# Loading k in 2 KB packets, like q, and turning it back on TensorE: a retention layer with routing on one Trainium2 core

## The chip, the cores and the metric

The kernel runs on one core of one Trainium2 chip. The metric is device time in microseconds (us) of one execution; lower is better. The engines are TensorE (PE in the profile, its weight loads PEld), VectorE (DVE), ScalarE (ACT), GpSimd (POOL) and SyncE (SP). SP issues most of the transfers, POOL the weight loads and the indirect transfers.

## The reference

Inputs are q, k and v, each 4 x 8 x 768 x 64 in float32 (4 batches, 8 heads, 768 tokens, head size 64), a gate vector of 512 and two weight matrices of 512 x 1024 and 1024 x 512. First comes a recurrent attention, then a small feed-forward network on the 128 best-scored tokens of each batch:

```python
gamma = 1.0 - 2.0 ** (-5.0 - np.arange(H))
for t in range(S):
    state = gamma * state + k_t (outer) v_t
    y[:, :, t] = scale * q_t @ state
# x = y with the heads side by side: (4, 768, 512)
scores = x @ w_gate
for b in range(B):
    top = the 128 tokens of the batch with the highest score
    h = relu(x[b, top] @ w1)
    out[b, top] = x[b, top] + sigmoid(scores[b, top]) * (h @ w2)
```

## The kernel before, in words

**Blocks.** A batch of 768 tokens is cut into 3 blocks of 256 tokens, which makes 12 blocks, m = 0 to 11. A block holds two chunks of 128 tokens, u = 0 and 1. The recurrence is computed by chunks: the scores of q and k inside a chunk, masked to the causal half and multiplied with v (`inside`), plus q times the state that the earlier chunks left (`across`). The state is kept in PSUM and a chunk's k and v are added to it (`update`); ScalarE copies it to SBUF for the next chunk.

**Loads.** `load(m)` issues on SP's queue, for one block, first q, then k, then v. q comes with 8 tokens of one head side by side in a partition, as runs of 8 x 64 float32, in two transfers (one for each parity of the head). k and v come with 2 tokens side by side, runs of 2 x 64 float32, in one transfer each. The pool `loads` has 5 buffers of each; blocks 0 to 3 are loaded ahead of the loop, block m + 4 at the start of iteration m.

**Casts.** `cast(m)` runs on POOL: q times its decay factors to `qb` (L184), k to bfloat16 `kb` (L186), v times its factors to `vb` (L187), in that order; iteration m casts block m + 2. The three results live in the pool `nats` with 5 buffers.

**Transposes.** `transposes(m, "q")` and `transposes(m, "k")` turn eight 128 x 128 tiles each on PE into the one PSUM tile `pt` (L196, L203; one buffer), and ScalarE copies it to `qT` (L198) or `kT` (L205). q's copy also sorts its tokens into natural order. k's layout, token pairs s and parity j, serves both as it is: `kb` has the tokens in the partitions, which is what the state update wants (L260), and `kT` has the head dimension there, which the scores want (L217).

**Scores.** `scores(m, part)` makes the products of four heads in the PSUM tile `pa` (one buffer), and DVE multiplies it with the causal mask into `am` (L220). `finish` copies the outputs to `xo` on ScalarE (L274) and forms the tokens' gate scores on DVE (`junk`, L277). `put` stores xo from SP's queue.

**Routing.** For each batch the rank of each token among all 768 is counted: `route_spread` (PE), `route_beats` (DVE comparisons, L312 to L319, into the tile `beats`), `route_ranks` (PE sums into two PSUM tiles `pk`), `route_index` (DVE; the tokens' numbers go into the tile `idx`, L354). Then `route_fetch` gathers the 128 rows with an indirect transfer on POOL (L360), `route_gate`, `route_turn` and `route_sigmoid` make the gate and the transposed rows, `ffn_up` and `ffn_down` are the network, `ffn_add` sums (L423), and `route_put` scatters the rows back with an indirect transfer on POOL (L428), which reads `idx` again. `idx`, `acc` and `gt` come from the pool `perb`, which has 2 buffers, so batch 2 takes the buffers of batch 0. The tiles of `route_spread`, `route_ranks`, `route_turn`, `ffn_up` and `ffn_down` share the tag "pm" of the PSUM pool `psM`, which has 2 buffers taken in turn.

**Order.** The order is written out by hand: each engine executes its instructions in the order of the program. The routing parts are put into numbered places of the iterations:

```python
for m in range(NBLK):
    load(m + 4); slot_work(m, -1); cast(m + 2)
    transposes(m + 1, "q"); scores(m, 1); update(m, 0)
    slot_work(m, 0); transposes(m + 1, "k"); slot_work(m, 1)
    py = inside(m); across(m, 0, py); across(m, 1, py)
    xo = finish(m, py); update(m, 1); put(m, xo)
    slot_work(m, 2); scores(m + 1, 0); slot_work(m, 3); slot_work(m, 4)
```

Batch b ends with block 3b + 2; its ranks are in place 3 and its index in place 4 of iteration 3b + 3. For batch 0 the fetch is in iteration 5 (place -1), the gate, turn and sigmoid in 7, the network in 8, the sum in 9 and `route_put(0)` in iteration 10 (place -1); batch 1 runs three iterations later, and batches 2 and 3 end in the places that follow the loop.

Of the kernel before, what the change touches and what calls it, by code (L numbers as in the profile page):

```python
# [9 lines left out]
FT = mybir.dt.float32  # L10
# [8 lines left out]
def kernel(ctx: ExitStack, tc: tile.TileContext, q, k, v, w_gate, w1, w2, capacity, out):  # L19
    nc = tc.nc  # L20
# [18 lines left out]
    consts = ctx.enter_context(tc.tile_pool(name="consts", bufs=1))  # L39
    loads = ctx.enter_context(tc.tile_pool(name="loads", bufs=5))  # L40
    work = ctx.enter_context(tc.tile_pool(name="work", bufs=3))
    nats = ctx.enter_context(tc.tile_pool(name="nats", bufs=5))
    store = ctx.enter_context(tc.tile_pool(name="store", bufs=4))
    perb = ctx.enter_context(tc.tile_pool(name="perb", bufs=2))
    psT = ctx.enter_context(tc.tile_pool(name="psT", bufs=1, space=bass.MemoryType.PSUM))
# [11 lines left out]
    def load(m):  # L57
        b, r = divmod(m, NM)
        for nm, src in (("q", q), ("k", k), ("v", v)):
            ap = src[b, :, r * T:(r + 1) * T, :]  # L60
            if nm == "q":
                t = loads.tile([128, 2, 8, D], FT, name="qf", tag="qf")
                for half in range(2):
                    nc.sync.dma_start(t[:, half].rearrange("p j d -> p (j d)"),
                                      bass.AP(tensor=ap.tensor, offset=ap.offset + half * S * D,
                                              ap=[[8 * D, T // 8], [2 * S * D, HP], [1, 8 * D]]))
            else:
                t = loads.tile([128, H, 2, D], FT, name=nm + "f", tag=nm + "f")
                ap = bass.AP(tensor=ap.tensor, offset=ap.offset, ap=[[2 * D, 128], ap.ap[0], [1, 2 * D]])
                nc.sync.dma_start(t.rearrange("p h j d -> p h (j d)"), ap)  # L70
            raw[nm, m] = t
# [106 lines left out]

    def cast(m):
        r = m % NM  # L180
        kb = nats.tile([128, 2, H, D], BF, name="kb", tag="kb")
        vb = nats.tile([128, 2, H, D], BF, name="vb", tag="vb")
        qb = nats.tile([128, 8, 2, D], BF, name="qb", tag="qb")
        nc.gpsimd.tensor_mul(qb, raw["q", m].rearrange("p h j d -> p j h d"),  # L184
                             gq[:, r, :, :, None].to_broadcast([128, 8, 2, D]))
        nc.gpsimd.tensor_copy(kb, raw["k", m].rearrange("p h j d -> p j h d"))  # L186
        nc.gpsimd.tensor_mul(vb, raw["v", m].rearrange("p h j d -> p j h d"),  # L187
                             gv[:, 2 * r:2 * r + 2, :, None].to_broadcast([128, 2, H, D]))
        nat[m] = (kb, vb, qb)

    def transposes(m, nm):
        src = nat[m][2 if nm == "q" else 0]
        if nm == "q":
            pt = psT.tile([128, 8, T // 8, HP], BF, name="pt", tag="pt")
            for i in range(8):
                nc.tensor.transpose(pt[:, i].rearrange("p s g -> p (s g)"), src[:, i], ident)  # L196
            t = work.tile([128, HP, T], BF, name="qT", tag="qT")
            nc.scalar.activation(t.rearrange("p g (s i) -> p g s i", i=8), pt.rearrange("p i s g -> p g s i"), AF.Copy)  # L198
        else:
            pt = psT.tile([128, 2, HP, 128], BF, name="pt", tag="pt")  # L200
            for j in range(2):
                for dd in range(HP):
                    nc.tensor.transpose(pt[:, j, dd, :], src[:, j, 2 * dd:2 * dd + 2, :], ident)  # L203
            t = work.tile([128, 2, HP, 128], BF, name="kT", tag="kT")
            nc.scalar.activation(t, pt, AF.Copy)  # L205
        tr[nm, m] = t

    def scores(m, part):
        qT, kT = tr["q", m], tr["k", m]
        pa = psA.tile([128, 2, 2, 2, C], FT, name="pa", tag="pa")  # L210
        for d in range(2):
            dd = 2 * part + d
            for j in range(2):
                for u in range(2):
                    for half in range(2):
                        r = slice(half * 64, half * 64 + 64)
                        nc.tensor.matmul(pa[u * 64:u * 64 + 64, half, d, j, :], kT[r, j, dd, u * 64:u * 64 + 64],  # L217
                                         qT[r, dd, u * C:(u + 1) * C], start=True, stop=True)
        am = work.tile([128, 2, 2, 2, C], BF, name="am", tag=f"am{part}")
        nc.vector.tensor_mul(am.rearrange("p a b c d -> p (a b) (c d)"), pa.rearrange("p a b c d -> p (a b) (c d)"),  # L220
                             causal.rearrange("p a b -> p (a b)")[:, None, :].to_broadcast([128, 4, 2 * C]))
        att[m, part] = am
# [24 lines left out]
    def update(m, u):  # L247
        i = 2 * m + u
        b, c = divmod(i, NC)
        if c == NC - 1:  # L250
            return
        kb, vb, _ = nat[m]
        if c == 0:
            pstate[b] = psS.tile([128, HP, D], FT, name="pst", tag="pst")
        r = slice(u * 64, u * 64 + 64)
        for dd in range(HP):
            for j in range(2):
                for half in range(2):
                    h = 2 * dd + half
                    nc.tensor.matmul(pstate[b][half * 64:half * 64 + 64, dd, :], kb[r, j, h, :], vb[r, j, h, :],  # L260
                                     start=(c == 0 and dd == 0 and j == 0), stop=True, skip_group_check=True)
        t = S_sb[(i + 1) % 2]
        for half in range(2):
            r = slice(half * 64, half * 64 + 64)
            nc.scalar.activation(t[r, :, half * 64:half * 64 + 64], pstate[b][r], AF.Copy)  # L265
# [26 lines left out]
    def route_spread(b, r):  # L292
        st = batch[b]
        if r == 0:
            st["row"] = perb.tile([128, S - T], FT, name="row", tag="row")
            st["beats"] = perb.tile([128, NC, S], BF, name="beats", tag="beats")
            st["won"] = perb.tile([128, NC], FT, name="won", tag="won")
        pr = psM.tile([128, 2, C], FT, name="pr", tag="pm")
        for u in range(2):
            c = 2 * r + u  # L300
            nc.tensor.transpose(pr[:, u, :], st["sc"][:, c:c + 1].to_broadcast([128, C]), identf)
        st["pr"] = pr
        if r < NM - 1:
            nc.scalar.activation(st["row"][:, r * T:(r + 1) * T], pr.rearrange("p u t -> p (u t)"), AF.Copy)
# [40 lines left out]

    def route_index(b):
        st = batch[b]
        acc = perb.tile([128, 2], FT, name="acc", tag="acc")
        for a, (lo, hi, pk) in enumerate(st["pk"]):
            junk = store.tile([128, 4 * C], BF, name="junki", tag="junki")  # L350
            nc.vector.scalar_tensor_tensor(junk[:, :(hi - lo) * C], pk.rearrange("p a t -> p (a t)"), slotcol[:, 0:1],
                                           tokrow[:, lo * C:hi * C], OP.is_equal, OP.mult, accum_out=acc[:, a:a + 1])
        idx = perb.tile([128, 1], I32, name="idx", tag="idx")
        nc.vector.tensor_scalar(idx, acc[:, 0:1], acc[:, 1:2], float(b * S), OP.add, OP.add)  # L354
        st["idx"] = idx

# [30 lines left out]
    def route_sigmoid(b):  # L387
        st = batch[b]
        if b < B - 1:
            ssel = perb.tile([128, 1], FT, name="ssel", tag="ssel")  # L390
            nc.scalar.activation(st["prod"], st["prod"], AF.Copy, accum_out=ssel)
        else:
            ssel = st["ssel"]
        e = perb.tile([128, 1], FT, name="e", tag="e")
        nc.scalar.activation(e, ssel, AF.Exp, scale=-1.0)
        e1 = perb.tile([128, 1], FT, name="e1", tag="e1")
        nc.vector.tensor_scalar_add(e1, e, 1.0)
        gt = perb.tile([128, 1], FT, name="gt", tag="gt")
        nc.vector.reciprocal(gt, e1)
        st["gate"] = gt  # L400

# [62 lines left out]
    transposes(0, "q")  # L464
    transposes(0, "k")
    scores(0, 0)

    for m in range(NBLK):
        if m + 4 < NBLK:
            load(m + 4)  # L470
        slot_work(m, -1)
        if m + 2 < NBLK:
            cast(m + 2)
        if 1 <= m < 5:
            load_weights(m - 1)
        if m + 1 < NBLK:
            transposes(m + 1, "q")
        scores(m, 1)
        update(m, 0)
        slot_work(m, 0)  # L480
        if m + 1 < NBLK:
            transposes(m + 1, "k")
        slot_work(m, 1)
        py = inside(m)
        for u in range(2):
            across(m, u, py)
        xo = finish(m, py)
        update(m, 1)
        put(m, xo)
        slot_work(m, 2)  # L490
        if m + 1 < NBLK:
            scores(m + 1, 0)
        slot_work(m, 3)
        slot_work(m, 4)
    for t, place in sorted(slots):
# [36 lines left out]
```

## Time and profile before

| | |
|---|---|
| median of 3 runs | 128.45 us (126.95, 132.09, 128.45) |
| profiled execution | 127.14 us, of which the span of instructions is 125.4 us |
| busy share of the span | PE 65%, PEld 51%, DVE 60%, ACT 53%, POOL 62% |
| moved by transfers | 29.87 MB, mean 238 GB/s; 34,273 packets |
| mean granted TensorE clock | 0.866 |

Busy is the time in which an engine executes something; an engine's idle time is put down to what ended it (the releaser). A window's row lists each engine's busy time in that stretch with the number of instructions, the granted clock, the mean busy share of the 16 DMA engines (over 1 when packets overlap) and the rate. "SPq" and "POOLq" are the queues' issuing instructions.

### The profile page before, as it was taken

How to read it: one execution, taken by the hardware profiler on the slowest of the kernel's cores; microseconds unless marked ns; L12 is line 12 of the kernel's file. 1: busy time of each engine (PE TensorE's matmuls, PEld its weight loads, DVE VectorE, ACT ScalarE, POOL GpSimd, SP SyncE). 2: the span in 40 equal slices, each digit the busy share in tenths (PEclk: the TensorE clock that was granted, in tenths of full speed). 3: DMA queues.
4: the chain of work that ended last, by engine and by line, in shares of the span. 5: the costliest groups of instructions: out<-in, count | busy, mean ns of one | idle time of the engine just before them, and what ended most of it. 6: DMA issues, size and time to landing. Idle time of an engine off the chain costs nothing. (4 is left out here: it accounts for less than half of the span.)

```text
span 125.4 us, 3891 instructions
## 1 busy us (share of the span) xinstructions
PE 81.3 (65%) x1605; PEld 64.0 (51%) x1612; DVE 75.1 (60%) x217; ACT 66.3 (53%) x129; POOL 77.3 (62%) x72
## 2 busy tenths in 40 slices
PE   0053775958499729349939499995438697785820
PEld 0041655847487518238637398664326683462600
DVE  6002353789899958708948668599165864934120
ACT  7133474987657739307619869467607543430500
POOL 6649999999853798480699969848940300330330
PEclk9999997799859995865799859999965579999995
DMA  2999999999999999999999999999406104203202
GB/s 63 282 335 304 344 304 324 310 309 317 246 310 257 368 295 255 337 244 325 363 336 314 334 351 332 299 315 391 170 25 200 56 5 167 84 0 84 84 0 84
DMA packets 34273, 29.87 MB, mean 238 GB/s; under 512 B 1360, under 2 KB 26960, under 8 KB 34256
## 3 DMA queue, kind: packets, MB, share of 16 engines
q1 hardware_dynamic: 32016, 25.43, 66.8%
q0 software_dynamic: 2240, 4.20, 14.8%
q8 instruction: 12, 0.20, 0.6%
q14 instruction: 5, 0.04, 0.1%
HBM read 24.38 MB, written 7.34 MB: 253 GB/s over the span
## 5 line engine op out<-in xcount | busy, mean ns | idle before, releaser
L220 DVE TENSOR_TENSOR am<-pa,causal 128x1024 bf16<-128x1024 f32 x24 | 29.3, 1222 | 23.6 <-PE pa L217 23.6
L187 POOL TENSOR_TENSOR vb<-vf,gv 128x1024 bf16<-128x1024 f32 x12 | 22.8, 1900 | 9.3 <-DMA vf<-in_v_dram 9.1
L184 POOL TENSOR_TENSOR qb<-qf,gq 128x1024 bf16<-128x1024 f32 x12 | 22.8, 1902 | 6.6 <-DMA qf<-in_q_dram 4.8
L198 ACT ACTIVATE qT<-pt 128x1024 bf16<-128x1024 bf16 x12 | 12.3, 1023 | 20.6 <-PE pt L196 20.6
L196 PE MATMUL pt<-ident,qb 128*128 128x128 bf16 x96 | 9.3, 255 | 20.7 <-POOL qb L184 20.7
L274 ACT ACTIVATE xo<-py 128x512 f32<-128x512 f32 x24 | 14.3, 597 | 13.0 <-DVE junk L277 7.2
L196 PEld LDWEIGHTS <-qb 128*128 128x128 bf16 x96 | 7.0, 114 | 22.2 <-POOL qb L184 21.7
L277 DVE SCALAR_TENSOR_TENSOR junk<-py,wgB 128x512 bf16<-128x512 f32 x24 | 15.6, 687 | 3.8 <-PE py L244 3.8
L217 PE MATMUL pa<-qT,kT 64*64 64x128 bf16 x384 | 12.5, 253 | 7.3 <-DVE am L220 5.9
L265 ACT ACTIVATE S<-pst 64x256 bf16<-64x256 f32 x40 | 15.0, 374 | 3.1 <-PE pst L260 2.6
L205 ACT ACTIVATE kT<-pt 128x1024 bf16<-128x1024 bf16 x12 | 12.3, 1022 | 2.9 <-PE pt L203 2.8
L428 POOL DMA_INDIRECT out_dram<-ye,idx x4 | 4.2, 1040 | 15.5 <-DVE ye L423 12.2
L217 PEld LDWEIGHTS <-kT 64*64 64x64 bf16 x384 | 8.5, 124 | 10.0 <-issue 6.9
L186 POOL CAST kb<-kf 128x1024 bf16<-128x1024 f32 x12 | 12.4, 1035 | 0.9 <-DMA kf<-in_k_dram 0.9
L234 PE MATMUL py<-vb,am 64*128 64x64 bf16 x384 | 10.0, 209 | 4.4 <-DVE am L220 4.4
L234 PEld LDWEIGHTS <-am 64*128 64x128 bf16 x384 | 8.1, 107 | 6.7 <-DVE am L220 4.7
L203 PE MATMUL pt<-ident,kb 128*128 128x128 bf16 x96 | 9.9, 264 | 1.5 <-ACT qT L198 1.4
L409 PE MATMUL ph<-xT,w1s 128*128 128x128 bf16 x128 | 9.8, 242 | 1.3 <-ACT xT L372 0.7
L260 PE MATMUL pst<-vb,kb 64*64 64x64 bf16 x320 | 10.4, 212 | 0.0
L203 PEld LDWEIGHTS <-kb 128*128 128x128 bf16 x96 | 8.6, 120 | 2.6 <-POOL kb L186 1.2
L409 PEld LDWEIGHTS <-w1s 128*128 128x128 bf16 x128 | 8.9, 110 | 1.7 <-issue 1.6
L260 PEld LDWEIGHTS <-kb 64*64 64x64 bf16 x320 | 8.8, 127 | 1.1 <-issue 0.6
(76 smaller groups left out, 123.1 us busy)
## 6 DMA issues: line engine op xcount, KB each, us to landing
qf<-in_q_dram SPq DMA_DIRECT2D x24, 256.0 KB, 6.0
kf<-in_k_dram SPq DMA_DIRECT2D x12, 512.0 KB, 7.6
vf<-in_v_dram SPq DMA_DIRECT2D x12, 512.0 KB, 8.5
out_dram<-xo SPq DMA_DIRECT2D x24, 256.0 KB, 4.8
w1s<-in_moe_w_dram POOLq DMA_DIRECT2D x2, 512.0 KB, 8.3
w2s<-in_moe_w_dram POOLq DMA_DIRECT2D x2, 512.0 KB, 10.1
wgB<-in_moe_w_gate_dram SPq DMA_DIRECT2D x1, 256.0 KB, 7.0
xg<-out_dram,idx POOLq DMA_INDIRECT x4, 5.5
```

The source lines that it names most:

```text
L184: nc.gpsimd.tensor_mul(qb, raw["q", m].rearrange("p h j d -> p j h d"), gq[:, r, :, :, None].to_broadcast([128, 8, 2, D]))
L187: nc.gpsimd.tensor_mul(vb, raw["v", m].rearrange("p h j d -> p j h d"), gv[:, 2 * r:2 * r + 2, :, None].to_broadcast([128, 2, H, D]))
L196: nc.tensor.transpose(pt[:, i].rearrange("p s g -> p (s g)"), src[:, i], ident)
L203: nc.tensor.transpose(pt[:, j, dd, :], src[:, j, 2 * dd:2 * dd + 2, :], ident)
L217: nc.tensor.matmul(pa[u * 64:u * 64 + 64, half, d, j, :], kT[r, j, dd, u * 64:u * 64 + 64], qT[r, dd, u * C:(u + 1) * C], start=True, stop ...
L220: nc.vector.tensor_mul(am.rearrange("p a b c d -> p (a b) (c d)"), pa.rearrange("p a b c d -> p (a b) (c d)"), causal.rearrange("p a b -> ...
L234: nc.tensor.matmul(py[u][:, h, :], att[m, dd // 2][r, half, dd % 2, j, :], vb[r, j, h, :], start=(h == 0 and j == 0), stop=True, skip_grou ...
L260: nc.tensor.matmul(pstate[b][half * 64:half * 64 + 64, dd, :], kb[r, j, h, :], vb[r, j, h, :], start=(c == 0 and dd == 0 and j == 0), stop ...
L265: nc.scalar.activation(t[r, :, half * 64:half * 64 + 64], pstate[b][r], AF.Copy)
L274: nc.scalar.activation(xo[:, u, :], py[u].opt(), AF.Copy)
L277: nc.vector.scalar_tensor_tensor(junk, py[w].opt(), 1.0, wgB, OP.mult, OP.mult, accum_out=batch[b]["sc"][:, 2 * r + w:2 * r + w + 1])
L409: nc.tensor.matmul(ph[:, j, :], w1s[:, dd, ff * 128:(ff + 1) * 128], st["xT"][:, dd, :], start=(j == 0 and dd == 0), stop=True, skip_group ...
```

## The change

k is loaded like q: 8 tokens side by side, runs of 8 x 64 float32, in two transfers a block. The cast keeps that layout (`kc`), and k takes the same transposes and the same sorting copy as q, so `kT` now has the tokens in natural order. The scores take the tokens of parity j out of kT with a step of 2 elements. The state update needs k with the tokens in the partitions, in pairs: `turn_back(m)` makes it out of kT with eight more PE transposes into a PSUM tile of the tag "pm" and one more ScalarE copy to `kb`. It stands after `scores(m, 0)`, ahead of the loop for block 0 and in iteration m - 1 for the others. `nats` has 4 buffers in place of 5, `beats` 1 in place of 2, `junki` 2 in place of 4; `acc`, `idx` and `gt` have 4 in place of 2.

```diff
-    nats = ctx.enter_context(tc.tile_pool(name="nats", bufs=5))
+    nats = ctx.enter_context(tc.tile_pool(name="nats", bufs=4))
...
-            if nm == "q":
-                t = loads.tile([128, 2, 8, D], FT, name="qf", tag="qf")
+            if nm != "v":
+                t = loads.tile([128, 2, 8, D], FT, name=nm + "f", tag=nm + "f")
                 for half in range(2):
                     nc.sync.dma_start(t[:, half].rearrange("p j d -> p (j d)"),
                                       bass.AP(tensor=ap.tensor, offset=ap.offset + half * S * D,
...
-        kb = nats.tile([128, 2, H, D], BF, name="kb", tag="kb")
+        kc = nats.tile([128, 8, 2, D], BF, name="kc", tag="kc")
...
-        nc.gpsimd.tensor_copy(kb, raw["k", m].rearrange("p h j d -> p j h d"))
+        nc.gpsimd.tensor_copy(kc, raw["k", m].rearrange("p h j d -> p j h d"))
...
     def transposes(m, nm):
         src = nat[m][2 if nm == "q" else 0]
...
+        pt = psT.tile([128, 8, T // 8, HP], BF, name="pt", tag="pt")
+        for i in range(8):
+            nc.tensor.transpose(pt[:, i].rearrange("p s g -> p (s g)"), src[:, i], ident)
+        t = work.tile([128, HP, T], BF, name=nm + "T", tag=nm + "T")
+        nc.scalar.activation(t.rearrange("p g (s i) -> p g s i", i=8), pt.rearrange("p i s g -> p g s i"), AF.Copy)
         tr[nm, m] = t
+
+    def turn_back(m):
+        pb = psM.tile([128, 2, HP, 128], BF, name="pb", tag="pm")
+        kT = tr["k", m].rearrange("p g (s j) -> p g s j", j=2)
+        for j in range(2):
+            for dd in range(HP):
+                nc.tensor.transpose(pb[:, j, dd, :], kT[:, dd, :, j], ident)
+        kb = work.tile([128, 2, H, D], BF, name="kb", tag="kb")
+        nc.scalar.activation(kb.rearrange("p j h d -> p (j h d)"), pb.rearrange("p j g x -> p (j g x)"), AF.Copy)
+        tr["kb", m] = kb
...
-                        nc.tensor.matmul(pa[u * 64:u * 64 + 64, half, d, j, :], kT[r, j, dd, u * 64:u * 64 + 64],
+                        nc.tensor.matmul(pa[u * 64:u * 64 + 64, half, d, j, :], kT[r, dd, u * C:(u + 1) * C].rearrange("p (s j) -> p s j", j=2)[:, :, j],
                                          qT[r, dd, u * C:(u + 1) * C], start=True, stop=True)
...
-        kb, vb, _ = nat[m]
+        kb, vb = tr["kb", m], nat[m][1]
...
-            st["beats"] = perb.tile([128, NC, S], BF, name="beats", tag="beats")
+            st["beats"] = perb.tile([128, NC, S], BF, name="beats", tag="beats", bufs=1)
...
-        acc = perb.tile([128, 2], FT, name="acc", tag="acc")
+        acc = perb.tile([128, 2], FT, name="acc", tag="acc", bufs=4)
...
-            junk = store.tile([128, 4 * C], BF, name="junki", tag="junki")
+            junk = store.tile([128, 4 * C], BF, name="junki", tag="junki", bufs=2)
...
-        idx = perb.tile([128, 1], I32, name="idx", tag="idx")
+        idx = perb.tile([128, 1], I32, name="idx", tag="idx", bufs=4)
...
-        gt = perb.tile([128, 1], FT, name="gt", tag="gt")
+        gt = perb.tile([128, 1], FT, name="gt", tag="gt", bufs=4)
...
     scores(0, 0)
+    turn_back(0)
...
             scores(m + 1, 0)
+            turn_back(m + 1)
```

More of the change, by code (lines that the diff above doesn't have):

```diff
@@ L185, in cast @@
                              gq[:, r, :, :, None].to_broadcast([128, 8, 2, D]))
-        nc.gpsimd.tensor_copy(kb, raw["k", m].rearrange("p h j d -> p j h d"))
+        nc.gpsimd.tensor_copy(kc, raw["k", m].rearrange("p h j d -> p j h d"))
         nc.gpsimd.tensor_mul(vb, raw["v", m].rearrange("p h j d -> p j h d"),
                              gv[:, 2 * r:2 * r + 2, :, None].to_broadcast([128, 2, H, D]))
-        nat[m] = (kb, vb, qb)
+        nat[m] = (kc, vb, qb)
     def transposes(m, nm):
         src = nat[m][2 if nm == "q" else 0]
[L193 to L205, printed above, removed]
-        tr[nm, m] = t
+        pt = psT.tile([128, 8, T // 8, HP], BF, name="pt", tag="pt")
[3 more added lines that the diff above has]
+        nc.scalar.activation(t.rearrange("p g (s i) -> p g s i", i=8), pt.rearrange("p i s g -> p g s i"), AF.Copy)
+        tr[nm, m] = t
+    def turn_back(m):
[7 more added lines that the diff above has]
+        tr["kb", m] = kb
     def scores(m, part):
```

## The prediction

> **What bounds the kernel now.** I read the windows of ten microseconds first, then the waits, then the timelines of POOL, DVE, ACT and PE around the longest waits. In the windows (length; busy us of PE, PEld, DVE, ACT, POOL with instruction counts; granted clock; DMA share; GB/s), transfers fill the 16 DMA engines until block 11 has landed, and no compute engine is full for long:
>
> ```profile
> 10.00:20.00 10.00, 5.40 (x132) 4.42 (x132) 4.90 (x7) 5.37 (x9) 9.86 (x11) 1.00 1.14 321
> 50.00:60.00 10.00, 6.23 (x114) 5.16 (x110) 5.91 (x15) 4.47 (x8) 4.62 (x5) 0.67 1.15 306
> 70.00:80.00 10.00, 8.78 (x152) 7.24 (x154) 6.53 (x17) 6.93 (x14) 8.66 (x7) 0.83 1.11 336
> 90.00:100.00 10.00, 5.53 (x100) 4.64 (x101) 6.07 (x14) 4.08 (x11) 3.52 (x3) 0.59 0.31 107
> ```
>
> The waits (engine and line, releaser: us in total, times, longest) say how that reaches the compute: PE waits for the cast of q, the cast waits for v's landing, and once DVE waits for a scatter:
>
> ```profile
> PE pt L196 <- POOL qb L184: 20.7, 7, 6.7
> POOL vb L187 <- DMA vf<-in_v_dram: 9.1, 7, 3.7
> ACT xo L274 <- DVE junk L277: 7.2, 11, 2.0
> DVE idx L354 <- DMA out_dram<-ye,idx: 3.4, 1, 3.4
> ```
>
> That last wait ties the end of the load stream to the tail. In POOL's timeline (start, us, engine, line) route_put(0) stands behind the cast of v of block 11; DVE, as its own timeline shows next, writes batch 2's index into batch 0's buffer only when that scatter has landed, and am of block 10 queues behind it:
>
> ```profile
> 86.75 1.90 POOL L187 TENSOR_TENSOR vb<-vf,gv 128x1024 bf16<-128x1024 f32 x1 [0.46 <-DMA vf<-in_v_dram]
> 88.81 1.08 POOL L428 DMA_INDIRECT out_dram<-ye,idx  x1 [0.16 <-issue]
> ```
>
> ```profile
> 88.24 0.09 DVE L351 DVE_READ_ACCUMULATOR junki<-pk,slotcol,tokrow 128x1 f32 x1
> 91.73 0.21 DVE L354 TENSOR_SCALAR idx<-acc 128x1 int32<-128x1 f32 x1 [3.41 <-DMA out_dram<-ye,idx]
> 91.86 1.22 DVE L220 TENSOR_TENSOR am<-pa,causal 128x1024 bf16<-128x1024 f32 x1
> ```
>
> Everything after 91.86 is a chain of compute and small transfers to 125.4. Where data are ahead, DVE sets the pace: from 24.85 to 44.26 it has hardly a gap but the 0.5 us in which PE refills pa. So the kernel is bound by loads only by a little, and what a faster load stream is worth depends on how little the extra work costs.
>
> **Loads.** The rows of the costs to add, and of SP's issues, are these (groups: count | busy us, mean ns of one):
>
> ```profile
> L205 ACT ACTIVATE kT<-pt 128x1024 bf16<-128x1024 bf16 x12 | 12.3, 1022 | 2.9 <-PE pt L203 2.8
> L203 PE MATMUL pt<-ident,kb 128*128 128x128 bf16 x96 | 9.9, 264 | 1.5 <-ACT qT L198 1.4
> kf<-in_k_dram SPq DMA_DIRECT2D x12, 512.0 KB, 7.6
> ```
>
> The trace's packet records hold, on SP's queue, 24,576 packets of 512 B (k and v), mean 31.0 ns, and 6,272 of 2 KB, mean 90.2 ns. A block of k is now 1,024 x 31.0 = 31.7 us of packet time and becomes 256 x 90.2 = 23.1: 8.65 less, over 16 engines 0.54, and over the share of 1.12 (packets overlap) 0.48 us. Fitting the packets that end in each half microsecond from 8 to 78 us gives 27 ns for one of 512 B and 86 for one of 2 KB: 1,024 x 27 - 256 x 86 = 5.6 us, over 16 engines 0.35. I take the middle, 0.41 us a block: 3.7 us at the landing of v of block 8 (9 blocks), 4.9 at that of block 11. SP issues one transfer more a block; an issue that isn't held up takes 0.6 us (median of k's 592 ns), and SP is idle or held up by a full queue for more than that in each iteration. Stores and the indirect fetches queue in the same stream and move up with it.
>
> The Trainium skill (DMA: Bandwidth & Descriptors, Specifications) puts the line rate at 512 B and up, which would make the saving nothing; the trace differs, since stretches of two microseconds with hardly any packet but 512 B move 303 to 325 GB/s and that from 86 us with 2 KB alone 397. By that rule the loads would give 0 in place of 3.7 us.
>
> **The index tiles.** The 3.41 us at 88.32 go: put(0) no longer holds idx. What is behind it moves up: am of block 10, then PE's inside(10) (idle 3.94 before its second half), ACT's xo (idle 4.15). fetch(2) waited 1.63 for this idx. Nothing else of batch 0 is then in DVE's way. I take 3.4; the bounds are 0 (another old reader holds DVE as long) and 3.4.
>
> **turn_back.** A block adds eight transposes, 0.62 us for a run of eight in the timeline at full granted clock and 1.03 at half, and one ACT copy, 1.02 (0.92 in a row of copies). That is 12 x 1.02 = 12.3 us on ACT (66.3 to 78.6) and 7.4 to 12.4 on PE. Behind the copy on ACT wait qT of the next block and, through it, PE's k transposes (pt has one buffer); behind PE's transposes wait the ranks, ffn_down or the next q transposes. By kind of iteration (iteration m turns back block m + 1):
> - Plain (m = 1, 2, 4, 5): ACT has the time where it waits, since DVE sets the pace. In iteration 2 the copy fits at 31.93 to 32.9, qT ends at 33.9, where ACT now waits 1.02 until 33.86 for pst: nothing. With a second state copy (0.77), as in iterations 1 and 4, the loop qT, k transposes, inside, across, junk, xo, state copy, kb is about 0.3 to 0.5 over DVE's. I take 0.3, 0.2, 0.5 and 0.1; bounds 0 and 0.92 each.
> - Ranks (m = 3, 6, 9): the two pk tiles take the pm buffers in turn after pr and pb, so the second waits until ACT has copied pb. ACT gets to it only after xo and the state copies; in iteration 3 at 39.07, so it ends at 40.1, and the second pk can't start at 38.6 but 1.5 us later. q's transposes queue behind it; am of the next block comes 0.8, inside 1.2 later. I take 1.0, 1.1 and 1.1; bounds 0.3 and 2.0.
> - Sigmoid (m = 7, 10): the copy stands between xT and prod on ACT, which is full there, and DVE waits for ACT's e before it goes on to am:
>
> ```profile
> 70.82 0.62 ACT L391 ACTIVATE prod<-prod 128x512 f32<-128x512 f32 x1
> 71.34 0.19 ACT L391 ACTIVATION_READ_ACCUMULATOR prod<-prod 128x1 f32 x1
> 71.56 0.20 ACT L395 ACTIVATE e<-ssel 128x1 f32<-128x1 f32 x1
> 72.09 1.02 ACT L198 ACTIVATE qT<-pt 128x1024 bf16<-128x1024 bf16 x1 [0.33 <-PE pt L196]
> ```
>
>   I take 1.0 and 1.1; bounds 0.5 and 1.1.
> - Network (m = 8): PE is busy 8.40 of the 8.45 us from 71.17 to 79.62, so its transposes count: 0.7; bounds 0.6 and 1.8, the upper one if the weight loads with a step of 2 elements are as slow as the float32 ones of the same 4 byte step (160 ns in place of 114, for 32 + 8 a block, less what lies under matmuls).
> Sum over iterations 1 to 10: 0.5 + 1.0 + 0.6 + 1.1 + 1.0 + 0.7 + 1.1 + 1.1 = 7.1 us; bounds 2.5 and 13.7.
>
> The step in the weight loads I cost at nothing elsewhere, under PE's idle third. The cast of k keeps its 1.04 us, and kT's copy takes the form of qT's (1,023 against 1,022 ns). nats with 4 buffers makes the cast of block m + 2 wait for the last read of block m - 2: for block 9 at 69.20 that was about 61.5, so nothing; with POOL held, PE's q transposes would be next. beats with one buffer: the ranks of batch 2 are read by 85.6, the next write is at 92.99: nothing. On step 2 the Trainium skill (SBUF — State Buffer, Door 1) lets bfloat16 step up to 8 elements free; no row of this trace shows it.
>
> **The sum.** I follow DVE's second mask of each iteration, which starts at 33.56 (iteration 3) and 72.68 (iteration 8). Without its waits for data the compute of iterations 3 to 7 is 7.2 + 5.25 + 6.6 + 7.3 + 6.45 = 32.8 of these 39.1 us (6.45 includes DVE's wait for e). The new start is 33.56 - 0.4 (one block of k sooner at the first casts) + 0.5 = 33.7. Compute then reaches iteration 8 at 33.7 + 32.8 + 3.7 = 70.2; data allow 72.68 - 3.7 = 69.0. The later holds: 2.5 us gained. Iterations 8 to 10 give back 0.7 + 1.1 + 1.1, the index wait gives 3.4, and the tail is as before: 2.5 - 2.9 + 3.4 = 3.0. The span becomes 122.4 and the profiled execution 127.14 - 3.0 = 124.1. The median of the three runs lies 1.3 above the profiled time and the runs spread over 5.1, so I add half of that, 0.7: **124.8 us**. A measurement of this kernel can tell about 2% from no change; 3.0 of 127.14 is 2.4%.
>
> **Rivals.**
> - *The copy hides and loads stay the bound.* ACT's 53% and its long idle stretches speak for it; the ranks' buffers and the sigmoid speak against. Then 3.7 + 3.4 = 7.1 less: 127.14 - 7.1 + 0.7 = 120.7.
> - *The load stream gains nothing.* POOL's casts, full from 11 to 34 us, speak for it, and the packet times may hold waiting that comes back elsewhere. Against it stands the higher rate of the 2 KB stretch. Data then allow 72.68, later than the compute's 70.2: 0 - 2.9 + 3.4 = 0.5 less, 127.3. An index wait that only changes its place ends near there too: 3.0 - 3.4, 128.2.
> - *The extra ACT copy becomes the bound* (the slower end). It is in order with qT, which starts each iteration; if each copy delays the loop in full (0.92 in the four plain iterations, 2.0 by ranks, the upper bounds elsewhere), 13.7 us replace 7.1 and the time is 127.14 - 3.0 + 6.6 + 0.7 = 131.4. It decides from additions of 10.1 us on, 1.0 an iteration. The single buffers of pt and pa speak for it, ACT's waits for others (20.6 us for pt alone) against.
>
> **Chances.** My forecast 0.45, of it 0.36 below the 2% line; the copy hidden 0.14; no gain from packets or the index 0.21, all within 2%; ACT the bound 0.20, all slower. Faster by over 2%: 0.36 + 0.14 = 0.50; within: 0.09 + 0.21 = 0.30; slower: 0.20. The forecast's own range is 122.5 to 127; for 8 in 10 it goes from 121.0, near the hidden copy, to 129.5, into the part of the slow case from which copies cost over 1.1 an iteration; outside lie about half of each of these two.
>
> **What would show it.** Right: packets under 2 KB down by 12,288; no wait of idx for out_dram; v of block 11 landing 4 to 5 us sooner; ACT near 78 us busy; the second pk waiting for ACT kb; PE's wait for qb well below 20.7. Wrong: PE's wait for qb still near 20 (loads not faster), or gone while am starts later than 72.68 in iteration 8 (copies cost more than walked), or DVE idle at batch 2's index for something else.

## The result, and the profile after

The changed kernel takes 123.13 us (median of 4 runs, 122.62 to 123.46) against 129.46 of the kernel before; the ratio is 0.964, with a 95% interval of 0.953 to 0.975. Its profiled execution took 123.08, the span is 121.4 in place of 125.4. Medians here hold all runs; the ratios leave out runs more than 1.5% slower than the fastest of the same kernel, so a ratio and the medians beside it can differ a little.

The windows of the kernel after (columns as before): transfers now fill the engines only to about 82 us, and the stretch after 90, which had a granted clock of 0.59, has 1.00.

```profile
80.00:90.00 10.00, 7.39 (x144) 6.02 (x145) 8.42 (x23) 5.80 (x11) 5.90 (x5) 0.83 0.36 136
90.00:100.00 10.00, 8.18 (x198) 6.49 (x196) 7.31 (x23) 8.06 (x18) 1.26 (x1) 1.00 0.27 92
```

The waits of the kernel after:

```profile
PE pt L195 <- POOL qb L184: 12.0, 4, 6.7
...
ACT xo L277 <- DVE junk L280: 6.5, 10, 2.0
POOL vb L187 <- DMA vf<-in_v_dram: 6.1, 4, 3.1
...
DVE e L400 <- ACT e L398: 4.7, 3, 1.9
PE pk L341 <- ACT kb L208: 4.5, 3, 1.9
```

PE's wait for qb fell from 20.7 to 12.0 and POOL's for v from 9.1 to 6.1; DVE's wait of idx for the scatter is gone. Two waits have taken part of their place, both behind the new copy on ACT: DVE's for e (before 1.8) and PE's second pk for kb. Of the other signs that were named, the packets of 512 B are half as many (all packets under 2 KB went from 26,960 to 14,864), and ACT is busy for 76.8 us where 78 had been said. From the groups (count | busy, mean of one | idle before) and the transfers:

```profile
L208 ACT ACTIVATE kb<-pb 128x1024 bf16<-128x1024 bf16 x12 | 12.3, 1022 | 1.8 <-PE pb L206 1.7
```

```profile
kf<-in_k_dram SPq DMA_DIRECT2D x24, 256.0 KB, 7.1
```

The copy costs what kT's did (1,022 ns each). The end of the load stream, in POOL's and DVE's timelines of the kernel after:

```profile
80.56 1.91 POOL L187 TENSOR_TENSOR vb<-vf,gv 128x1024 bf16<-128x1024 f32 x1
82.63 1.08 POOL L431 DMA_INDIRECT out_dram<-ye,idx  x1 [0.16 <-DVE beats L315]
```

```profile
87.76 0.22 DVE L357 TENSOR_SCALAR idx<-acc 128x1 int32<-128x1 f32 x1
88.68 1.23 DVE L223 TENSOR_TENSOR am<-pa,causal 128x1024 bf16<-128x1024 f32 x1 [0.70 <-PE pa L220]
```

The last cast of v starts 6.2 us sooner, batch 2's index is written without a wait, and the mask that follows starts 3.2 sooner than 91.86.

The prediction was made in the start of "the second mask of an iteration". Exactly, it is the mask of `scores(m, 1)`, the second of block m, which DVE makes in iteration m. From the DVE timelines (us), with two kernels of the experiments beside the two:

| iteration | 3 | 4 | 5 | 6 | 7 | 8 | 9 | 10 | 11 | span |
|---|---|---|---|---|---|---|---|---|---|---|
| before | 33.56 | 40.76 | 47.42 | 56.82 | 65.76 | 72.68 | 80.63 | 91.86 | 98.91 | 125.4 |
| after | 33.21 | 41.11 | 46.63 | 56.46 | 64.35 | 71.58 | 79.24 | 88.68 | 96.19 | 121.4 |
| no turn_back | 34.19 | 41.39 | 46.63 | 56.78 | 63.98 | 70.01 | 77.09 | 84.95 | 91.47 | 117.1 |
| weights in 1, 4, 5, 6 | 32.79 | 40.68 | 46.37 | 52.30 | 60.19 | 67.42 | 75.08 | 84.09 | 91.95 | 117.7 |

### The profile page after: what moved, and what is told of

The parts are those of the page before. It is cut to its first block, busy times and chain, and to the rows that moved or that the text cites. A ratio compares the mean times of both kernels' runs of the same rounds, so it can differ in the third digit from the quotient of the medians.

```text
span 121.4 us, 4113 instructions
## 1 busy us (share of the span) xinstructions
PE 83.1 (68%) x1701; PEld 64.9 (53%) x1708; DVE 75.0 (62%) x217; ACT 76.8 (63%) x141; POOL 77.2 (64%) x72
## 2 busy tenths in 40 slices
DMA packets 25250, 29.88 MB, mean 246 GB/s; under 512 B 1552, under 2 KB 14864, under 8 KB 25232
## 5 line engine op out<-in xcount | busy, mean ns | idle before, releaser
L197 ACT ACTIVATE qT<-pt 128x1024 bf16<-128x1024 bf16 x12 | 12.3, 1022 | 14.3 <-PE pt L195 14.3
L220 PE MATMUL pa<-qT,kT 64*64 64x128 bf16 x384 | 11.7, 243 | 5.6 <-DVE am L223 4.0
L186 POOL CAST kc<-kf 128x1024 bf16<-128x1024 f32 x12 | 12.4, 1036 | 1.6 <-DMA kf<-in_k_dram 1.6
L208 ACT ACTIVATE kb<-pb 128x1024 bf16<-128x1024 bf16 x12 | 12.3, 1022 | 1.8 <-PE pb L206 1.7
L263 PE MATMUL pst<-vb,kb 64*64 64x64 bf16 x320 | 9.5, 203 | 1.6 <-ACT kb L208 1.6
L195 PE MATMUL pt<-ident,kc 128*128 128x128 bf16 x96 | 8.8, 244 | 2.0 <-ACT qT L197 1.6
L341 PE MATMUL pk<-beats,ones 128*128 128x512 bf16 (+3 forms) x29 | 5.8, 304 | 6.0 <-ACT kb L208 4.5
L237 PE MATMUL py<-vb,am 64*128 64x64 bf16 x384 | 9.0, 198 | 1.0 <-issue 0.6
L195 PEld LDWEIGHTS <-kc 128*128 128x128 bf16 x96 | 7.6, 111 | 3.6 <-issue 2.5
L263 PEld LDWEIGHTS <-kb 64*64 64x64 bf16 x320 | 7.8, 118 | 3.2 <-ACT kb L208 2.3
L363 POOL DMA_INDIRECT xg<-out_dram,idx x4 | 4.3, 1084 | 8.1 <-PE pa L220 3.8
```

Of the source, the lines that this page charges most:

```text
L186: nc.gpsimd.tensor_copy(kc, raw["k", m].rearrange("p h j d -> p j h d"))
L208: nc.scalar.activation(kb.rearrange("p j h d -> p (j h d)"), pb.rearrange("p j g x -> p (j g x)"), AF.Copy)
```

## The experiments

**The parts of the change, apart.** The theory was that the change holds two gains, the index wait and the load stream, and one cost, the turned-back copies. The rivals were that one of the gains is all, that the copy hides, or that ACT becomes the bound. Four kernels make or undo one part each. The kernels of the experiments ran in three groups on three chips (these four; the first edits of the weights and the copies; the loads by themselves and those with the weights in 1, 4, 5 and 6), and each ratio is against the kernel before on the same chip; spans are of one profiled execution, and across the groups they compare less well.

*The buffer counts alone*, in the kernel before:

```diff
-        idx = perb.tile([128, 1], I32, name="idx", tag="idx")
+        idx = perb.tile([128, 1], I32, name="idx", tag="idx", bufs=4)
...
```

> The kernel before with the change's buffer counts alone (nats 4, beats 1, junki 2; acc, idx, gt 4); k stays in 512 B packets and is not turned back. Theory 1 (index wait and load stream are two separate gains, the turned-back copies a cost of some 3 us): the 3.4 us wait of DVE for the scatter goes, the span becomes 122.0, 2.7% faster. Rival A (fewer nats or beats buffers hold POOL or DVE): 125.4 or more, with a new wait of qb or beats. Rival B (the index wait only covered other waits): 124.5 to 125.4.

Measured: 123.52 us, ratio 0.973 (0.952 to 0.993), span 122.1 at a mean granted clock of 0.85. DVE writes the index of batch 2 at 89.04, straight after what stands before it, and POOL issues the scatter at 88.08:

```profile
88.92 0.08 DVE L351 DVE_READ_ACCUMULATOR junki<-pk,slotcol,tokrow 128x1 f32 x1
89.04 0.21 DVE L354 TENSOR_SCALAR idx<-acc 128x1 int32<-128x1 f32 x1
89.17 1.21 DVE L220 TENSOR_TENSOR am<-pa,causal 128x1024 bf16<-128x1024 f32 x1
```

From the second mask of iteration 9 to that of iteration 10 it takes 7.9 us (81.31 to 89.17) where the kernel before takes 11.2. So in the kernel before that wait was on the path. Its waits show no new one for a smaller buffer count.

*Two index tiles again*, in the kernel after:

```diff
-        idx = perb.tile([128, 1], I32, name="idx", tag="idx", bufs=4)
+        idx = perb.tile([128, 1], I32, name="idx", tag="idx")
...
```

> The changed kernel with two tiles each of acc, idx and gt again. By the prediction's sum, which adds the index wait as a term of its own, the 3.4 us come back: span 124.8. By the trace of the changed kernel they don't: the scatter of batch 0 is issued at 82.63 there and lands some 3 us later, at about 85.5, while DVE reaches the index of batch 2 only at 87.76; then the span stays at 121.4 within 0.3, and the faster loads alone had taken that wait away.

Measured: 122.86 us, ratio 0.972 (0.943 to 1.000), span 120.7. The interval is too wide to decide by time; the profile does. Its POOL and DVE timelines:

```profile
83.01 1.08 POOL L431 DMA_INDIRECT out_dram<-ye,idx  x1 [0.16 <-issue]
```

```profile
86.90 0.21 DVE L357 TENSOR_SCALAR idx<-acc 128x1 int32<-128x1 f32 x1
```

The scatter is issued 3.9 us ahead of the index, enough for it to land (2.8 us in the kernel before), and there is no wait. With k in 2 KB packets the four index tiles are worth nothing: either the four tiles or the sooner loads take the 3.4 us away. The prediction's sum counts the 3.4 us once, so its total isn't hurt, but it gives them to one edit alone.

*No turn_back*, in the kernel after:

```diff
-        pb = psM.tile([128, 2, HP, 128], BF, name="pb", tag="pm")
...
+        kb = nat[m][0].rearrange("p i b d -> p (i b d)").rearrange("p (j h d) -> p j h d", j=2, h=H)
         tr["kb", m] = kb
```

> The changed kernel without turn_back: the state update takes the cast k in the order in which it was loaded (so the state sums pair wrong tokens; all else is computed as before), with no transposes to pb and no copy of it. Theory 1: the turned-back copies cost about 3 us in iterations 7 to 10, where loads no longer set the pace, and little before: span 118 to 118.5, the second pk and DVE's wait for e back at their old places. Rival (the copies hide): 121 to 121.4. Rival (ACT is the bound all along): 114 to 116.

Measured: 119.38 us, ratio 0.945 (0.919 to 0.972), span 117.1. Turning back costs 4.3 us of span in the profiles (3.6 against the kernel with two index tiles, which ran on the same chip), more than the 3 expected and less than if ACT were the bound. The table shows where: up to iteration 6 nothing (56.46 against 56.78, data set the pace), then, as differences of the steps from one iteration to the next, 0.7 in iteration 6, 1.2 in 7 (sigmoid), 0.6 in 8 (network), 1.6 in 9 (ranks) and 1.0 in 10 (sigmoid).

*turn_back alone*, with k in 512 B packets, in the kernel of the buffer counts:

```diff
+    def turn_back(m):
...
+                nc.tensor.transpose(pb[:, j, dd, :], kT[:, j, dd, :], ident)
...
-        kb, vb, _ = nat[m]
+        kb, vb = tr["kb", m], nat[m][1]
```

> The kernel before with the change's buffer counts and with turn_back, but k loaded in 512 B packets as before (the turned-back k is computed and used). Theory 1: index wait gone, -3.4, copies +2.9 in iterations 8 to 10 and hidden before by the waits for data: span 124.5 to 125.5, no faster than before; so the packets are worth 3.5 to 4 us in the changed kernel. Rival (packets worth nothing, the index tiles are the gain): 121.4, as the changed kernel. Rival (ACT the bound): 127 or more.

Measured: 125.67 us, ratio 0.994 (0.987 to 1.001), span 124.6, in the range of the first theory. So turning back costs about 2.1% of the time before with small packets (0.994 against 0.973) and 1.9% with large ones (0.964 against 0.945), and the packets gain 2.8% without turning back (0.973 to 0.945) and 3.0% with it (0.994 to 0.964). The intervals of these ratios are 0.7 to 2.6% to either side, so each difference is good to a per cent or two. The spans, one profile each, give 3.2 us for the packets with turning back (124.6 to 121.4), a little less than the 3.5 to 4 expected.

**The packets by themselves.** A kernel that does nothing but load k's 12 blocks in 512 B packets and then in 2 KB ones:

> Nothing but loads of k: 12 blocks in 512 B packets, then the same 12 in 2 KB packets, on SP's queue, into tiles of their own; the output is filled with sums that mean nothing. Theory (packet size is what the load stream gains by, as the fit of the packet records gave 27 and 86 ns): 12 blocks of 512 B take 12 x 1,024 x 27 / 16 = 20.7 us (304 GB/s), the same in 2 KB 12 x 256 x 86 / 16 = 16.5 us (381 GB/s). Rival (512 B is at the line rate when nothing runs beside): both take the same time, within 3%.

Its windows (in this kernel busy time is of DVE and POOL alone; then clock, DMA share, GB/s), the first of 512 B packets, the second of 2 KB:

```profile
5.00:15.00 10.00, 1.35 (x6) 0.00 (x0) 1.00 1.20 290
...
30.00:40.00 10.00, 1.58 (x7) 0.00 (x0) 1.00 1.05 386
```

290 and 386 GB/s in the one run: the large packets are a third faster, with nothing beside them. The two kinds of load also differ in the number of transfers (12 of 512 KB, 24 of 256 KB) and in which tokens a partition takes, as they do in the change, so the size of the packets by itself isn't shown to be the cause. Per packet that is 28.2 and 84.9 ns of one of 16 engines, 0.45 us for a block of k; the prediction took 0.41. The line rate that the Trainium skill (DMA: Bandwidth & Descriptors, Specifications) gives from 512 B on isn't reached at 512 B here.

**What became of the gain at block 6.** The prediction let the data of every block come sooner in proportion. The trace after shows otherwise. POOL's timeline before, and after:

```profile
43.48 0.80 POOL L168 DMA_DIRECT2D w2s<-in_moe_w_dram  x1
...
47.78 1.90 POOL L187 TENSOR_TENSOR vb<-vf,gv 128x1024 bf16<-128x1024 f32 x1 [0.46 <-DMA vf<-in_v_dram]
```

```profile
39.42 0.80 POOL L168 DMA_DIRECT2D w2s<-in_moe_w_dram  x1
42.73 1.89 POOL L184 TENSOR_TENSOR qb<-qf,gq 128x1024 bf16<-128x1024 f32 x1 [2.51 <-DMA qf<-in_q_dram]
44.59 1.03 POOL L186 CAST kc<-kf 128x1024 bf16<-128x1024 f32 x1
48.74 1.90 POOL L187 TENSOR_TENSOR vb<-vf,gv 128x1024 bf16<-128x1024 f32 x1 [3.13 <-DMA vf<-in_v_dram]
```

v of block 6 comes 1.0 us later than before (47.78), and PE then waits 4.2 us for q of block 7. The new theory was that POOL, held up less, issues the weights sooner too (39.42 in place of 43.48), so that they run beside block 6's loads. The packet records fit it: POOL loads w1 and w2 in two halves each, of 0.52 MB, and a half takes some 3 us of the 16 engines (256 packets of mean 183 ns or 512 of mean 99); when the cast of v of block 6 began, 1.18 MB of the weights had moved in the kernel before and 1.56 in the kernel after. The edit moves them:

```diff
-        if 1 <= m < 5:
-            load_weights(m - 1)
+        if m in (1, 5, 6, 7):
+            load_weights((1, 5, 6, 7).index(m))
```

> The changed kernel with the four weight loads of POOL issued in iterations 1, 5, 6 and 7 in place of 1 to 4. Theory 2 (the packets' gain was lost at block 6 because the weight loads, issued sooner too, run beside its loads): v of block 6, which POOL awaited until 48.7, lands 3 us or more sooner, PE's idle 4.2 us before the q transposes at 54.8 shrink to under 2, and the span falls by 1 to 3 us, to 118.4 to 120.4. Rival (only the sum of the bytes counts; blocks 8 to 10 wait in place of 6 and 7): 121.0 to 122.

Measured: 125.66 us, ratio 0.986 (0.976 to 0.995), span 124.1: slower than the kernel after, by 2.7 us of span, so the forecast of 118.4 to 120.4 missed. The theory's first half holds, for POOL starts v of block 6 at 42.57 and the second mask of iteration 8 starts at 68.17 in place of 71.58. The loss is a new wait, in PE's timeline of this kernel:

```profile
73.10 1.02 PE L420 MATMUL pd<-w2s,hT 128*128 128x512 bf16 x3 [0.67 <-ACT hT L414]
78.64 1.86 PE L420 MATMUL pd<-w2s,hT 128*128 128x512 bf16 x4 [4.52 <-DMA w2s<-in_moe_w_dram]
```

POOL issued the last half of w2 only at 68.24, behind the cast of v of block 9:

```profile
68.24 0.81 POOL L168 DMA_DIRECT2D w2s<-in_moe_w_dram  x1
```

With the iterations 1, 4, 5 and 6 in its place:

> The changed kernel with the weight loads in iterations 1, 4, 5 and 6. In the run with 1, 5, 6 and 7 the second mask of iterations 6 to 8 came 3.4 us sooner, and then PE stood 4.5 us for the second half of w2, which POOL issued at 68.24. Theory 2 (loads beside the weight transfers set the pace in iterations 4 to 6, and the late w2 alone made that run slower): the half of w2 issued at about 57 lands by 68, PE doesn't wait for it, and 2 to 3.4 us stay to the end: span 118 to 119.5. Rival (later weights only move the wait to blocks 8 to 10): PE or POOL waits for blocks 8 or 9 as long as it waited for block 6, span 121.4 or more.

Measured: 120.52 us, ratio 0.949 (0.941 to 0.957), span 117.7; the kernel after, measured again on the same chip, gave a ratio of 0.964 (0.957 to 0.970):

> The changed kernel itself again, as the measure for the two others on the same chip: span 121 to 122 where PE's clock is granted at 0.94 or more.

Its median was 123.47 us, and its spans went from 120.2 to 123.1 (122.5 in the profile), more spread than expected, at clocks from 0.919 to 0.961. In the profile of the kernel with the weights in 1, 4, 5 and 6 PE has no wait for w2, and row four of the table shows 4.2 us gained at iteration 6 and kept. So with the weights out of the way the data of blocks 6 and 7 come sooner. That the change lost its gain there because the weights were issued sooner is argued from the times and bytes above: no run moved the weights in the kernel before, so how much the same move would gain with 512 B packets isn't known.

**Two waits behind the copy.** The second pk waits for the pm buffer that pb holds:

```diff
-            pk = psM.tile([128, hi - lo, C], FT, name="pk", tag="pm")
+            pk = (psY if lo else psM).tile([128, hi - lo, C], FT, name="pk", tag="py0" if lo else "pm")
```

> The changed kernel with the second tile of the ranks (pk of chunks 4 and 5) in the PSUM buffer of py0 in place of the pm buffers, so that it no longer waits for ACT's copy of pb. Theory 1 (that wait is a good part of what turning back costs): PE's wait of pk for kb (4.5 us in three iterations) goes, the q transposes behind it come 1.2 to 1.8 sooner in iterations 3, 6 and 9, and the span falls by 1 to 2 us, to 119.4 to 120.4. Rival (DVE and ACT set the pace there, PE's wait is beside the path): 121.4 within 0.4.

Measured: 122.34 us, ratio 0.958 (0.949 to 0.967): the interval holds the ratio of the kernel after, so the whole time doesn't tell. Its profiled execution was the longest of its five, with a span of 123.8 where 119.4 to 120.4 had been expected. In that profile no wait of pk for kb is left, and from iteration 9 to 10 it takes 7.9 us where the kernel after takes 9.4, at a lower mean clock (0.916 for 0.955). The other edit makes two of the copies on DVE:

```diff
+        if m in (8, 11):
+            nc.vector.tensor_copy(kb.rearrange("p j h d -> p (j h d)"), pb.rearrange("p j g x -> p (j g x)"))
+        else:
+            nc.scalar.activation(kb.rearrange("p j h d -> p (j h d)"), pb.rearrange("p j g x -> p (j g x)"), AF.Copy)
```

> The changed kernel with the copies of pb for blocks 8 and 11 (iterations 7 and 10, where the sigmoid stands behind them on ACT) made by DVE in place of ACT. Theory 1 (the copy delays ACT's e, and DVE waits for e before its next mask): e comes 0.9 sooner, DVE's copy fits into its wait of 1.9, about 0.8 in each of the two iterations: span 119.8 to 120.6. Rival (DVE's copy only takes the place of the wait): 121.4 or more.

Measured: 123.04 us, with runs from 120.94 to 124.89: inconclusive by time. Its profile, of span 121.5, has 6.3 us from iteration 7 to 8 where the kernel after has 7.2, and no gain from 10 to 11. All three edits together, first with the weights in 1, 5, 6 and 7:

> The changed kernel with all three edits: the second ranks tile in py0, the weight loads in iterations 1, 5, 6, 7, and the two copies on DVE. Theory: the gains mostly add, span 116.5 to 118, about that of the changed kernel with no turn_back (117.1). Rival (each of the three uncovers the next wait): 119.5 or more.

Measured: 125.33 us, ratio 0.984 (0.975 to 0.993), span 123.4. This missed for the reason above: PE waits 8.3 us for w2, which POOL issued at 69.3. Then with the weights in 1, 4, 5 and 6:

> The kernel of i_weights_1456 with the second ranks tile in py0 and the copies of blocks 8 and 11 on DVE as well. If the three waits (data in iteration 6, pk for kb, DVE for e) are separate: span 115 to 117, below the changed kernel with no turn_back (117.1). Rival (once data are ahead, DVE or PE set the pace and the two small edits are worth nothing): 118 to 119.5, as i_weights_1456.

Measured: **117.36 us**, ratio 0.922 (0.916 to 0.929), span 114.7, a little below what was expected. The rival falls: beside the moved weights the two small edits are worth 3.0 us of span (117.7 to 114.7). From iteration 6 to 7, 7 to 8 and 9 to 10 this kernel takes 7.2, 6.0 and 7.9 us, just what the kernel with no turn_back takes there, where the kernel of the weights alone takes 7.9, 7.2 and 9.0. So the wait of pk and that for e are what turning back costs in those iterations; iteration 8, with 8.6 us, became 1.0 longer than with the weights alone, for a cause that wasn't looked for. No wait of pk for kb is in its waits, and those for qb and e (12.0 and 4.7 in the kernel after) are shorter:

```profile
PE pt L195 <- POOL qb L184: 9.9, 5, 6.6
...
DVE e L403 <- ACT e L401: 1.5, 3, 0.8
```

This is the fastest kernel of the study.

## Why the prediction was right, step by step

Forecast were 124.8 us, 3.0 off the span, and 121.0 to 129.5; measured were 123.13 and 4.0. The mechanism was right in the main: faster loads, DVE's wait for the scatter gone, and part of the gain given back by copies behind which ranks, sigmoid and network wait. Term by term, in the measure of the second masks:

- **Loads.** 0.41 us a block was near (0.45 alone). v of block 11 was to land 4.9 us sooner and its cast started 6.2 sooner. The step that failed is that each block gains in proportion: at block 6 the gain was lost, by the times and bytes to the weights that were issued sooner too, so iteration 6 began with data and not, as in the sum, with compute, and 1.1 us were gained at iteration 8 in place of 2.5. One reading behind the term compared unlike things: the stretch from 86 us, 397 GB/s with 2 KB packets, holds stores of xo, for the last load had landed by 86.75. The loads alone, at 386 GB/s, bear its conclusion out.
- **turn_back.** 7.1 us had been summed over iterations 1 to 10. Against the kernel with no turn_back the plain iterations cost about what was walked (0.3 in iteration 4 where 0.5 were taken for it). The ranks cost 0.7 (iterations 3 and 6) and 1.6 (9) where 1.0 to 1.1 were taken: the wait of the second pk was found where it was foretold, and in iteration 3 it ends at 39.82 after 1.47 us, where 40.1 had been worked out. Sigmoid and network cost 1.2, 1.0 and 0.6 for 1.0, 1.1 and 0.7.
- **The index tiles.** The 3.4 us went, as in the sum, but the reason given was not the only one: the sooner loads would have taken the wait away without the four tiles. The rival in which an index wait only changes its place fell too.
- **Tail.** Taken as unchanged; from the second mask of iteration 11 to the end it is 25.2 in place of 26.5 us, and iteration 8 took 7.7 in place of 8.0 with the copy in it. Both ran at a higher granted clock: 0.98 for 0.89 in the tail, 1.00 for 0.87 in iteration 8. The other profiles say the same of the tail, which does nearly the same work in all of them: 25.2 to 25.4 us in the five with a clock of 0.94 to 0.99 there, 25.6 to 27.1 in the seven with 0.88 to 0.93 (the kernel with the weights in 1, 4, 5 and 6 lies between, 25.75 at 0.96). No run changed the clock alone. The balance is then 1.4 less than forecast at iteration 8, 1.1 more in iterations 8 to 10 and 1.3 more in the tail. Neither gain is a term of the sum, so that the number came within 1.0 us of span is in part luck.
- **The 0.7 us** added for the median wasn't needed: the four runs after spread over 0.8 us, and their median is the profiled run's time.

Of the rivals, the one with no gain from the loads falls by the loads alone and by the packets' part of the ratio, 0.994 against 0.964 with turning back (the intervals don't meet); the one with ACT as the bound by the kernel with no turn_back, which starts iteration 6 no sooner. The copy doesn't hide either: 4.3 us of span.

## What to carry to other kernels

Before two waits are summed as two gains, ask whether the first edit moves the second wait's releaser: here either of two edits took the wait away. A faster stream also makes the engine that issues other transfers run ahead, so look at what it issues sooner and next to which load (here moving three weight loads was worth 1.5% of the time, 0.964 to 0.949, and 3.7 us of span in the profiles, 121.4 to 117.7). Here a new user of a PSUM tag with two buffers showed up as a wait of a later user of the tag (pk, 4.5 us in three places), and cost what stood queued behind that one.

## What the hardware showed that I had not expected

In these traces the granted clock goes with PE's gaps. Between 20 us and the end of the loop the clock records of the kernel before have six stretches at half clock, from 20.2, 33.8, 47.5, 54.3, 71.4 and 91.9 us; next to each stands a wait of PE of 1.7 to 3.9 us, which ended at 20.18, 33.09, 46.40, 55.16, 71.17 and 93.13 (one of 2.05, which ended at 64.74, has none). The kernel after has two, from 52.3 and 86.5, beside waits of 4.2 and 1.9 us which ended at 54.80 and 86.50. Over all runs the kernel before had mean clocks of 0.81 to 0.92, the kernel after 0.92 to 0.96, and the fastest kernel had 0.98 in its profile. After the 4.2 us wait of iteration 6, eight transposes take 1.03 us in place of 0.62:

```profile
54.80 1.03 PE L195 MATMUL pt<-ident,qb 128*128 128x128 bf16 x8 [4.18 <-POOL qb L184]
```

So here a wait of PE cost again in the instructions behind it. PE's busy time grew by only 1.8 us (81.3 to 83.1) with 96 transposes more, while its other matmuls became shorter (those of py 198 ns in the mean for 209, of pst 203 for 212); that the clock is the reason is argued. The loads in 512 B packets reach 290 GB/s by themselves and those in 2 KB 386; and weight loads with a step of 2 elements (kT in the scores) are no slower than contiguous ones: 118 ns in the mean at a clock of 0.955, where the kernel before had 124 at 0.866 and the kernel with turn_back alone, contiguous, 120 at 0.943.
